# Centroids turned raw and scaled in place, first loads on two queues, and a new order of the early work

## The chip, the cores and the metric

The kernel runs on one core of a Trainium2 chip. The metric is the device time of one execution in microseconds (us). Three runs of the kernel before gave 226.42, 226.63 and 226.57 us, median 226.57 us. One more execution was profiled; it took 227.3 us, of which the profile's span covers 225.3 us.

## The reference

Tokens attend only to tokens of the same cluster; the cluster is the nearest of 16 centroids of the head by cosine. Its output goes through a feed-forward layer (softmax-linear activation, normalisation, output product).

```python
c_n = centroids / (np.linalg.norm(centroids, axis=-1, keepdims=True) + 1e-06)
q_assign = np.argmax(np.einsum('bhsd,hcd->bhsc', q_n, c_n), axis=-1)
k_assign = np.argmax(np.einsum('bhsd,hcd->bhsc', k_n, c_n), axis=-1)
mask = q_assign[:, :, :, None] == k_assign[:, :, None, :]
scores = np.where(mask, scale * np.matmul(q, k.transpose(0, 1, 3, 2)), -1000000000.0)
attn = softmax(scores)
x = (attn @ v), heads side by side          # 3072 tokens x 512
h = x @ w_in                                # 512 x 1024
solu = h * softmax(h)
out = (layernorm(solu) * g_ln) @ w_out      # 1024 x 512
```

Batch 4, 8 heads, 768 tokens, head size 64, all in float32.

## The kernel before

The work goes by head pairs: 4 batches of 4 pairs, named `b.p`. For each pair the kernel loads q and k rows (`raw`), turns them so that the 64 head components lie on partitions (`xt`), multiplies them with the normalised centroids (`csc`, the "cluster product"), turns that back (`cst`), takes the maximum per token (`mx`), makes a one-hot row (`oh`), turns it again (`oht`) and copies it into 16 partitions below the cast q and k in `qk`. With these rows under them the score product `sps` gives masked scores in one pass. ACT takes the exponential (`e`), PE multiplies with v (`ops`), DVE divides by the sum (`x`), and the feed-forward layer follows for 128 tokens at a time (`hreg`, `u`, `yps`).

Nothing is scheduled by the compiler. Every step has a short name and stands in a table (`ORDER`), one list per engine, written out by hand; a second table (`AWAY`) says which steps run on an engine other than their usual one. Each engine issues its list strictly in that order, and semaphores make a step wait for its inputs. The names that matter here:

- `cn`: the norms of the 128 centroid rows, and before the change the scaled rows `c_n` (L877 to L890). `cp`: PE turns `c_n` into `cps` (L899). `cf`: DVE multiplies that with a 0/1 mask `own` into `c_by_two` (L903), the centroid operand of the first five pairs, which lies in `w_out_c`. `cq`, `cb`: the same again into `c_bd` (L910), for the later pairs.
- `tp`: three transposes of q or k on PE into one of three banks of `hreg` (L402); `xa`: the copy of such a bank to `xt` (L409), by DVE or ACT. A fourth `tp` must wait until the `xa` of the first has emptied its bank.
- `ca`: the casts into `qk` (L454 to L458). `cl`: the cluster product (L471). `tb`, `mx`, `oh`, `ot`: its way back (L485, L498, L504, L520). `pl`: the copy of the one-hot rows into `qk` (L532).
- Pair 0.0 is done in halves: the first head's tokens run through `tp`, `cl` to `pl` alone, so that its scores can begin before the second head is ready. The halves are called 0 and 1 below.
- `S`, `E`, `V`, `N`: one bank of scores (two matmuls, L637), its exponential (L643), one value product (six matmuls, L660), one division (L685). Scores have three PSUM banks, so the fourth S waits for the first E.
- `wm` and `fl`: matmuls on zeros whose result is not used (`idle_p`, L854). They stand where PE would wait otherwise.
- `gt` (L594): a small transpose that stands after the 14th S; here it is a milestone, since all that follows it stands in the same order in both kernels.

Of the kernel before, what the change touches and what calls it, by code (L numbers as in the profile page):

```python
# [22 lines left out]
class Weave:  # L23
# [6 lines left out]
        ld4 lv si ld6 lv ld lg lv ld2 lo2 lv lo ld2 lo ld6 li4 tx ld lv ld6 lv tx lv tu ld5 lv ld tx  # L30
        ld tu ld tu ld8 ou ld tu ou ld4 lv ld7 lv ld tu ld4 ou tx ld tu ld4 ou tx ld5 ou ld tu ld2
        lv ld tu ld tx ld4 ou ld3 ou pl ld5 tu lv ld4 lv tu ou tu ld3 lv ou tx ld lv tu ld2 pl ou tx
        ld2 ou pl tu ou lv tx tu pl ou tu2 tx2 tu ou tx2 tu ou tu ou tx tu ou tu ou tu ou6
    """
    ORDER["POOL"] = """
        zo po =ca0.0.0.1.0 ca =pl0.0.0.1.1 pl cv =ca0.1.0.1 =ca0.1.0.0 =pl0.0.1.0.0 pl z
        =pl0.0.1.0.1 ca pl ca =cv0.1.1 =ca0.2.1.1 pl =ca0.2.0.1 pl2 ca2 =ca0.3.1.1 cv =pl0.2.0.0
        =ca0.3.1.0 cv pl =ca0.3.0.1 z pl =cv0.3.1 =ca1.0.0.0 cv =ca1.0.1.0 pl =z4 gs z ca =pl1.0.1.1
        sg ca =pl1.0.0.1 pl2 wi4 =ca1.1.1.0 =cv1.0.1 =ca1.1.0.1 cv =ca1.1.1.1 =at1 =ca1.2.0.1 at ca
        al =pl1.1.1.1 cv =pl1.1.0.0 pl bl pl ca z =ca1.2.1.1 al at ca cv =pl1.2.1.1 =pl1.2.0.0 al  # L40
        =pl1.2.0.1 pl =ca2.0.1.0 bl cv =ca1.3.0.1 at =cv1.3.1 =ca1.3.1.0 ca al =pl1.3.1.1 =pl1.3.0.0
        pl cv bl pl =cv2.1.0 ca =pl2.0.0.0 pl =at5 pl2 at al =ca2.0.1.1 =ca2.1.0.0 =pl2.1.0.1
        =ca2.1.1.1 ca cv al =ca2.3.0.0 bl cv =pl2.1.1.1 =ca2.2.0.1 =ca2.1.1.0 =pl2.1.0.0 =ca2.2.0.0
        pl bl =ca2.3.1.1 at2 al =ca2.2.1.0 cv ca cv pl =ca2.3.1.0 pl at pl =pl2.3.1.1 =pl2.3.1.0 ca
        pl at pl al =ca3.0.0.0 ca =ca3.0.1.0 bl ca =cv2.3.1 al =ca3.1.1.1 cv =pl3.0.0.0 =pl3.0.1.1
        pl bl =ca3.2.0.1 al ca =cv3.0.1 cv pl at2 ca al =pl3.1.1.1 =ca3.3.0.0 =ca3.2.0.0 =cv3.1.1
# [5 lines left out]
        wm fl2 tp fl2 tp fl8 cp tp fl7 cl tp fl11 cl fl16 tp S tp S cq S2 tp S tp2 S V S tp V S tp  # L52
# [33 lines left out]
    """  # L86
    AWAY = {}
    AWAY.update(dict.fromkeys("""
        ca0.0.0.0.0 ca0.0.0.1.1 ca1.3.1.1 sc23.0 tu22.1 tu23.1 xa0.0.1.0 xa0.2.1.0 xa0.2.1.1
        xa0.3.0.0  # L90
    """.split(), "ACT"))
    AWAY.update(dict.fromkeys("""
# [1203 lines left out]
```

## Time and profile before

| what | value |
|---|---|
| median of three runs | 226.57 us |
| profiled execution, whole | 227.3 us |
| its span | 225.3 us |
| PE busy | 219.2 us (97%) |
| DVE busy | 200.3 us (89%) |
| ACT busy | 191.3 us (85%) |
| POOL busy | 127.7 us (57%) |
| first score matmul starts | 10.82 us |
| first exponential starts | 11.25 us |

The share of busy time is counted for each engine by itself. PE means matmuls, PEld the loading of their weights, DVE the vector engine, ACT the scalar engine, POOL the GpSimd engine, SP the engine that issues most DMAs; a name with q (SPq, ACTq) is the time that an engine spends on issuing a DMA. The chain of waits is followed back from the last instruction, and shows at each moment what the end was waiting for. In the timeline the columns are start, duration, engine, line, operation, what it writes and reads, and in brackets how long the engine had been idle and who released it. A matmul's duration in the timeline includes its pipeline, so neighbours overlap; the chain of waits shows only the part that moves the end.

### The profile page before, as it was taken

To read this page: it belongs to the slowest core of one execution; us is meant where nothing else is said; L and a number is where in the kernel's file an instruction comes from. 1 tells how busy PE (TensorE), PEld (TensorE's weight loads), DVE (VectorE), ACT (ScalarE), POOL (GpSimd) and SP (SyncE) were. 2 spreads that over 40 slices of the span, in tenths; PEclk is the share of its full clock that TensorE was granted. 3 is DMA by queue.
4 is the path that set the end of the run, shared out by engine and by line. 5 is a ranking of instruction groups with operands and counts; after the bars stand their busy time and mean duration, and the time that the engine had idled before them with its cause. 6 is when DMAs were issued, how large, how long until landed. Compare 5 with 4: busy or idle time off the path is not lost.

```text
span 225.3 us, 6745 instructions
## 1 busy us (share of the span) xinstructions
PE 219.2 (97%) x2501; PEld 146.8 (65%) x2501; DVE 200.3 (89%) x359; ACT 191.3 (85%) x366; POOL 127.7 (57%) x246
## 2 busy tenths in 40 slices
PE   8999999999999999999999999999999999999993
PEld 8877864666666767666566656676666677665452
DVE  2799997899999999999999899898998996879982
ACT  3399988999979999998989979899989899964353
POOL 3379985942385597289995670957965102122341
PEclk9999999999999999999999999999999999999999
DMA  5999994289999999799997998789771724659522
GB/s 182 366 370 354 196 243 191 47 163 220 187 179 153 213 179 169 148 161 175 184 219 155 147 215 149 180 170 162 175 166 58 93 28 116 90 155 177 166 83 103
DMA packets 117327, 38.80 MB, mean 172 GB/s; under 512 B 105640, under 2 KB 112816, under 8 KB 117296
## 3 DMA queue, kind: packets, MB, share of 16 engines
q1 hardware_dynamic: 117008, 38.06, 79.0%
q8 instruction: 19, 0.31, 0.6%
q10 hardware_dynamic: 288, 0.33, 0.4%
q14 instruction: 12, 0.10, 0.2%
HBM read 23.11 MB, written 6.29 MB: 130 GB/s over the span
## 4 chain that ended last, share of the span: by engine, by line
PE 80%; DVE 10%; ACT 2%; POOL 2%; issue 2%; DMA 1%; SPq 1%; DVEq 0%; ACTq 0%; POOLq 0%
PE sps L637 23%; PE hreg L746 16%; PE yps L810 16%; PE ops L660 12%; PE hreg L402 3%; PE csc L476 3%; PE idle_p L854 3%; DVE xt L427 2%; ACT e L643 2%; PE csc L471 1%; DMA raw<-in_q_dram 1%; DVE nmax L752 1%; DVE y L827 1%; DVE oh L510 1%; PE hreg L609 1%
## 5 line engine op out<-in xcount | busy, mean ns | idle before, releaser
L643 ACT ACTIVATE e<-sps 128x512 bf16<-128x512 f32 x288 | 150.6, 610 | 10.5 <-PE sps L637 8.6
L637 PE MATMUL sps<-qk 80*128 80x256 bf16 (+3 forms) x648 | 98.9, 260 | 0.3
L637 PEld LDWEIGHTS <-qk 80*128 80x128 bf16 (+1 forms) x648 | 52.1, 97 | 32.0 <-issue 8.6
L660 PEld LDWEIGHTS <-e 128*128 128x128 bf16 x1152 | 52.5, 97 | 16.0 <-issue 4.0
L660 PE MATMUL ops<-v,e 128*128 128x65 bf16 x1152 | 58.7, 193 | 0.5 <-DVE x L685 0.3
L746 PE MATMUL hreg<-w_in_sb,xT 128*128 128x512 bf16 x192 | 54.4, 379 | 0.0
L810 PE MATMUL yps<-w_out_c,uT 128*128 128x512 bf16 x184 | 49.9, 379 | 0.3 <-DVE y L827 0.3
L765 DVE TENSOR_TENSOR u<-e_sb,hreg 128x1024 bf16<-128x1024 bf16 (+1 forms) x25 | 29.1, 1166 | 5.0 <-ACT e_sb L758 4.9
L758 ACT ACTIVATE e_sb<-hreg,nmax 128x1024 bf16<-128x1024 f32 x24 | 26.8, 1118 | 6.7 <-DVE nmax L752 6.5
L776 DVE BATCH_NORM_STATS2 bs<-u 128x6 f32<-128x512 bf16 x48 | 31.6, 676 | 0.3
L550 POOL COPY qk<-oht 32x384 f32<-32x384 f32 x40 | 20.6, 515 | 18.8 <-DVE oht L523 14.9
L752 DVE TENSOR_REDUCE nmax<-hreg 128x1 f32<-128x1024 f32 x24 | 28.9, 1203 | 1.3 <-PE hreg L746 1.1
L456 POOL CAST qk<-xt 64x768 bf16<-64x768 f32 (+1 forms) x31 | 25.5, 823 | 6.9 <-DVE xt L409 3.0
L458 POOL TENSOR_SCALAR qk<-xt 64x768 bf16<-64x768 f32 (+1 forms) x28 | 23.4, 836 | 4.0 <-PE yps L810 2.3
L810 PEld LDWEIGHTS <-uT 128*128 128x128 bf16 x200 | 17.8, 97 | 11.5 <-ACT uT L742 0.8
L746 PEld LDWEIGHTS <-xT 128*128 128x128 bf16 x192 | 16.5, 97 | 8.1 <-issue 0.6
L792 POOL TENSOR_SCALAR esq<-es,mv 128x1 f32<-128x1 f32 x24 | 8.1, 339 | 22.6 <-DVE mv L780 22.0
L427 DVE STREAM_TRANSPOSE xt<-raw 128x768 f32<-128x768 f32 x22 | 20.9, 959 | 0.0
L685 DVE TENSOR_TENSOR x<-ops,den 128x256 bf16<-128x256 f32 (+1 forms) x39 | 18.9, 486 | 1.3
L786 POOL TENSOR_SCALAR es<-esum 128x1 f32<-128x1 f32 x24 | 5.6, 239 | 23.3 <-ACT e_sb L758 14.9
L568 POOL CAST v<-vf 128x384 bf16<-128x384 f32 x27 | 14.3, 532 | 7.7 <-DMA vf<-in_v_dram 4.7
L795 POOL TENSOR_TENSOR alpha<-esq,halves 128x1 f32<-128x1 f32 x24 | 13.4, 560 | 2.0
(82 smaller groups left out, 186.6 us busy)
## 6 DMA issues: line engine op xcount, KB each, us to landing
vf<-in_v_dram SPq DMA_DIRECT2D x16, 384.0 KB, 4.4
out_dram<-y SPq DMA_DIRECT2D x23, 256.0 KB, 2.8
raw<-in_q_dram SPq DMA_DIRECT2D x44, 96.0 KB, 3.2
raw<-in_k_dram SPq DMA_DIRECT2D x44, 96.0 KB, 3.4
w_g<-in_moe_w_out_dram SPq DMA_DIRECT2D x4, 512.0 KB, 8.0
w_st<-in_moe_w_in_dram SPq DMA_DIRECT2D x4, 512.0 KB, 6.9
raw<-in_q_dram SPq DMA_DIRECT2D x4, 384.0 KB, 7.2
raw<-in_k_dram SPq DMA_DIRECT2D x4, 384.0 KB, 7.8
```

The source lines that it names most:

```text
L427: nc.vector.transpose(xt[:], raws[b, p, i][:].rearrange("p j c -> p (j c)"))
L456: VEC[e].tensor_copy(dst, src)
L458: VEC[e].tensor_scalar(dst, src, scalar1=inv_C, scalar2=1.0, op0=Alu.mult, op1=Alu.mult)
L637: nc.tensor.matmul(sps_[n, k][:, c0:c0 + w], side(b, h // 2, 1, h % 2, keys)[r], side(b, h // 2, 0, h % 2, slice(s0 * P, s0 * P + w))[r])
L643: nc.scalar.activation(es[n, k][:, :w], sps_[n, k][:, :w], Act.Exp, scale=exp_scale, bias=-exp_scale)
L660: nc.tensor.matmul(opss[g][:, s, :VW], es[n, k][:, c0:c0 + P], v1[slot(b, h // 2)][:, h % 2, kt, :VW], start=(kt == 0), stop=(kt == n_t - 1))
L746: uses(nc.tensor.matmul(hreg[:, at(f, f2)[1], :], xTs[f][:, dc, :], w_in_sb[:, dc, f2 * FF2:(f2 + 1) * FF2], start=(dc == 0), stop=(dc == ...
L752: uses(nc.vector.tensor_reduce(ff[f, "nmax"][:], pair_of(f), axis=AXY, op=Alu.max, negate=True), *both(f))
L758: uses(nc.scalar.activation(ff[f, "e"][:], pair_of(f), Act.Exp, bias=ff[f, "nmax"][:], accum_out=ff[f, "esum"][:]), *both(f))
L765: uses(nc.vector.tensor_tensor(ff[f, "u"][:, at_], ff[f, "e"][:, at_], pair_of(f)[:, at_], op=Alu.mult), *banks)
L776: nc.vector.bn_stats(ff[f, "bs"][:, f2, :], ff[f, "u"][:, f2, :])
L810: ins = nc.tensor.matmul(dst, ff[f, "uT"][:, at(f, f2)[0] * (n_fc // 2) + c, :], w_out_c[:, fc, cols], start=(fc == chunks[0]), stop=(fc = ...
```

## The change

The centroids are no longer scaled before they are turned. Their 128 raw rows are loaded twice, side by side, one copy by SP's queue and one by ACT's. PE turns them as soon as they are there; ACT copies the result to SBUF (`ct`, tile `c_t`). The norms run beside that. PE then multiplies a 128x128 broadcast of the inverse norms with the identity, which spreads them along the free axis on all partitions (`ci`). DVE multiplies both into the blocks of `c_by_two` and `c_bd` that are not zero; POOL has zeroed the whole tiles before. The blocks of heads 0 and 1 come first (`cg`), those of heads 2 to 7 (`cf`) and `c_bd` (`cb`) later. One small DVE step of the norm now does not depend on the one in front of it. The scaled rows `c_n`, the mask `own`, the second transpose `cq` are gone. Core of the diff:

```diff
-    nc.sync.dma_start(out=c_all[:], in_=centroids.rearrange("h c d -> (h c) d"))
+    for x, e in enumerate((nc.sync, nc.scalar)):
+        e.dma_start(out=c_two[:, x, :], in_=centroids.rearrange("h c d -> (h c) d"))
     for hh in range(2):
         for i in range(2):
-            load_head(0, 0, i, hh, nc.sync if i or hh else nc.scalar)
+            load_head(0, 0, i, hh, nc.sync if i else nc.scalar)
...
+    nc.gpsimd.memset(c_by_two, 0.0)
+    nc.gpsimd.memset(c_bd[:], 0.0)
...
-    nc.vector.scalar_tensor_tensor(out=c_r0[:], in0=c_r0[:], scalar=c_nsq[:], in1=c_s0[:],
+    nc.vector.tensor_scalar(c_s1[:], c_s0[:], scalar1=2e-6, scalar2=None, op0=Alu.add)
+    nc.vector.scalar_tensor_tensor(out=c_norm[:], in0=c_r0[:], scalar=c_nsq[:], in1=c_s1[:],
                                    op0=Alu.mult, op1=Alu.add)
-    nc.vector.tensor_scalar(c_norm[:], c_r0[:], scalar1=0.5, scalar2=1e-6,
-                            op0=Alu.mult, op1=Alu.add)
     nc.vector.reciprocal(c_inv[:], c_norm[:])
-    nc.vector.tensor_scalar(c_n[:], c_all[:].unsqueeze(1).to_broadcast([P, 2, D]),
-                            scalar1=c_inv[:], scalar2=None, op0=Alu.mult)
-    add("wm", "PE", 3.55, -1000, lambda e: [idle(P) for _ in range(26)])
+    add("wm", "PE", 3.55, -1000, lambda e: [idle(P) for _ in range(18)])
...
+    def spread_inverse():
+        nc.tensor.matmul(cs["t"][:, 1, :], c_inv[:].to_broadcast([P, P]), ident_f[:])
+
+    def keep_blocks(dst, lo, hi, step):
+        for x in range(2):
+            r = slice(x * D, (x + 1) * D)
+            src = [y.rearrange("p (h c) -> p h c", c=NC_) for y in (c_t[r], cs["t"][r, 1, :])]
+            hs = slice(lo + (x if step == 2 else 0), hi, step)
+            nc.vector.tensor_tensor(dst[r, :, x * NC_:(x + 1) * NC_], src[0][:, hs], src[1][:, hs],
+                                    op=Alu.mult)
+
+    add("cp", "PE", 0.42, 0, lambda e: turn_centroids(), [])
+    add("ct", "ACT", 0.3, -600, lambda e: nc.scalar.copy(c_t[:], cs["t"][:, 0, :]), ["cp", "wa"])
+    add("ci", "PE", 0.42, 0, lambda e: spread_inverse(), ["cn", "cp"])
+    add("cg", "DVE", 0.25, -500, lambda e: keep_blocks(c_by_two[:, 0:2], 0, 2, 1), ["ci", "ct"])
+    add("cf", "DVE", 0.3, -490, lambda e: keep_blocks(c_by_two[:, 2:H], 2, H, 1), ["ci", "ct"])
+    add("cb", "DVE", 0.3, -480, lambda e: keep_blocks(c_bd[:], 0, H, 2), ["ci", "ct"])
```

The turned centroids and the spread norms share the PSUM tile of the value products (`ops`), so the first V now waits for `cf` and `cb`. A `pl` of half 0 and one `xa` of half 1 go to ACT; the one-hot step takes its engine from the table, and still runs on DVE everywhere. The tables move the early work, up to `gt`; behind it all lists are as before. The start of PE's list before and after:

```diff
-        wm fl2 tp fl2 tp fl8 cp tp fl7 cl tp fl11 cl fl16 tp S tp S cq S2 tp S tp2 S V S tp V S tp
-        cl V S tp2 S V S2 V tp S V S gt tp S2 cl S2 V2 S V S tp S V S V S tp S V S cl S2 V S V3 S2
+        wm fl2 cp fl6 tp2 ci tp fl2 cl tp fl8 cl fl10 S2 tp2 S2 tp4 S3 tp cl tp S2 V tp S V3 S2 V tp
+        S V S gt tp S2 cl S2 V2 S V S tp S V S V S tp S V S cl S2 V S V3 S2 tp2 S V S V2 S tp S V S2
```

First place, ACT's list from its start. Before it issues one load, and copies three of the four `hreg` banks of pair 0.0:

```order
L384 DMA raw<-in_q_dram 128x384
L860 ACT_TABLE_LOAD
L860 ACTIVATE warm<-halves 128x1
L409 COPY xt<-hreg 128x384 x3
L454 ACTIVATE qk_99<-xt 64x3x128 x2
L643 ACTIVATE e<-sps 128x512 x6
L454 ACTIVATE qk_99<-xt 64x3x128 x2
L643 ACTIVATE e<-sps 128x512
L409 COPY xt<-hreg 128x384
```

After the change:

```order
L842 DMA c_two<-in_centroids_dram 128x64
L382 DMA raw<-in_q_dram 128x384 x2
L861 ACT_TABLE_LOAD
L861 ACTIVATE warm<-halves 128x1
L916 COPY c_t<-cps 128x128
L407 COPY xt<-hreg 128x384 x2
L452 ACTIVATE qk_99<-xt 64x3x128
L407 COPY xt<-hreg 128x384 x2
L452 ACTIVATE qk_99<-xt 64x3x128
L536 COPY qk_99<-oht 16x2x3x64
L452 ACTIVATE qk_99<-xt 64x3x128
L643 ACTIVATE e<-sps 128x512 x4
```

ACT now issues three loads ahead of its table load, copies all four banks of pair 0.0 and the turned centroids, and takes one `pl` (L536) from POOL.

Second place, DVE's list from the `pl` of half 0 to the copies of pair 0.1. Before:

```order
L532 COPY qk_99<-oht 16x2x3x32 x2
L485 STREAM_TRANSPOSE cst<-csc 128x192
L409 COPY xt<-hreg 128x384
L498 TENSOR_REDUCE mx<-cst 128x12
L409 COPY xt<-hreg 128x384
L910 TENSOR_TENSOR c_bd<-cps,own 128x128
L568 CAST v_0_105<-vf 128x6x64
L504 TENSOR_TENSOR w_out_c<-cst,mx 128x6x2x16
L409 COPY xt<-hreg 128x384
L520 STREAM_TRANSPOSE oht<-w_out_c 128x384
L409 COPY xt<-hreg 128x384 x3
```

After the change:

```order
L536 COPY qk_99<-oht 16x2x3x32 x2
L483 STREAM_TRANSPOSE cst<-csc 128x192
L911 TENSOR_TENSOR w_out_c<-c_t,cps 64x6x16 x2
L911 TENSOR_TENSOR c_bd<-c_t,cps 64x4x16 x2
L496 TENSOR_REDUCE mx<-cst 128x12
L407 COPY xt<-hreg 128x384 x4
L502 TENSOR_TENSOR w_out_c<-cst,mx 128x6x2x16
L568 CAST v_0_105<-vf 128x6x64
L518 STREAM_TRANSPOSE oht<-w_out_c 128x384
L407 COPY xt<-hreg 128x384 x2
```

Six copies stand there in both. Four small block products (L911) take the place of one product (L910), and four copies now stand in a row ahead of the one-hot step of half 1.

Third place, PE's list from its first scores. Before:

```order
L402 MATMUL hreg<-ident_f,raw 128x128 x3
L637 LDWEIGHTS qk_99
L637 MATMUL sps<-qk_99 128x256
L637 LDWEIGHTS qk_99
L637 MATMUL sps<-qk_99 128x256
L402 MATMUL hreg<-ident_f,raw 128x128 x3
L637 LDWEIGHTS qk_99
L637 MATMUL sps<-qk_99 128x256
L637 LDWEIGHTS qk_99
L637 MATMUL sps<-qk_99 128x256
L899 MATMUL cps<-ident_f,c_n 128x128
```

After the change, from the third score bank on (two banks and two `tp` stand ahead):

```order
L637 LDWEIGHTS qk_99
L637 MATMUL sps<-qk_99 128x256
L637 LDWEIGHTS qk_99
L637 MATMUL sps<-qk_99 128x256
L637 LDWEIGHTS qk_99
L637 MATMUL sps<-qk_99 128x256
L637 LDWEIGHTS qk_99
L637 MATMUL sps<-qk_99 128x256
L400 MATMUL hreg<-ident_f,raw 128x128 x12
```

The scores now go in twos and threes, and four `tp` (12 transposes) stand in one row, which is more than the three banks hold.

More of the change, by code (lines that the diff above doesn't have):

```diff
@@ L38 @@
[L38 to L43, printed above, removed]
@@ L1037 @@
                 e = ("DVE", "POOL")[j % 2] if half else "POOL" if apart(b, p) else "SP"
-                costs = ({"DVE": 0.3, "POOL": 0.41} if half else
+                costs = ({"DVE": 0.3, "POOL": 0.41, "ACT": 0.46} if half else
                          {"POOL": 0.76, "DVE": 0.46} if apart(b, p) else
@@ L1226 @@
             add(f"ou{f}", "SP", 0.54, s + 8, (lambda e, f=f: f_out(f)), [f"sc{f}"], move=0.8)
-    for name, eng, busy in (("cn", "DVE", 4.66), ("wa", "ACT", 4.3), ("po", "POOL", 3.7),
+    for name, eng, busy in (("cn", "DVE", 4.66), ("po", "POOL", 3.7),
                             ("si", "SP", 3.95)):
```

159 lines of the change are left out of this document (76 added, 83 removed).

## The prediction

> **What bounds the kernel now.** First the page, for the share of each engine:
>
> ```profile
> span 225.3 us, 6745 instructions
> PE 219.2 (97%) x2501; PEld 146.8 (65%) x2501; DVE 200.3 (89%) x359; ACT 191.3 (85%) x366; POOL 127.7 (57%) x246
> ```
>
> PE is nearly full, but part of its early work is filler, so the share alone says nothing of the start. There the chain of waits is read (start, length, what):
>
> ```profile
> 0.97 3.17 PE idle_p L854 x28
> ...
> 4.14 0.64 PE hreg L402 x3
> ...
> 4.99 0.64 PE hreg L402 x3
> 5.63 0.85 PE idle_p L854 x8
> 6.49 0.21 PE cps L899
> 6.70 0.41 PE hreg L402 x3
> ...
> 7.50 0.46 PE csc L471 x8
> ...
> 8.44 0.61 PE idle_p L854 x11
> 9.05 0.47 PE csc L471 x8
> ...
> 10.53 0.33 PE hreg L402 x3
> 10.86 0.35 PE sps L637 x2
> ...
> 11.54 0.22 PE sps L637 x2
> ...
> 19.50 0.15 PE gps L594
> 19.65 0.48 PE hreg L402 x3
> ```
>
> The chain stays on PE, but up to 10.53 us it is mostly fillers: PE waits there for data, in disguise. What follows stands in a fixed order; a lead won before 10.5 us reaches the end if every engine that is full in between can take it. The windows tell who is full (us from:to, length, then busy time of PE, PEld, DVE, ACT, POOL):
>
> ```profile
> 10.50:19.40 8.90, 8.90 (x104) 6.96 (x102) 8.70 (x18) 8.03 (x17) 6.91 (x13) 1.00 1.08 361
> 19.40:26.10 6.70, 6.70 (x87) 4.72 (x87) 6.09 (x14) 6.65 (x14) 6.18 (x10) 1.00 1.04 302
> 26.10:34.70 8.60, 8.22 (x125) 6.24 (x124) 8.28 (x19) 7.78 (x16) 7.61 (x16) 1.00 0.90 227
> ```
>
> PE is busy all the time to 26.1 us, and DVE for 8.70 of 8.90 us in the first of these: two engines carry the early stage together. DVE's timeline gives the rest:
>
> ```profile
> 4.70 0.16 DVE L889 RECIPROCAL c_inv<-c_norm 128x1 f32<-128x1 f32 x1
> ...
> 6.74 0.42 DVE L903 TENSOR_TENSOR w_out_c<-cps,own 128x256 f32<-128x256 f32 x1
> ...
> 8.03 0.38 DVE L485 STREAM_TRANSPOSE cst<-csc 128x192 f32<-128x192 f32 x1 [0.33 <-PE csc L471]
> ...
> 9.92 0.58 DVE L532 COPY qk<-oht 16x192 f32<-16x192 f32 x2
> 10.53 0.38 DVE L485 STREAM_TRANSPOSE cst<-csc 128x192 f32<-128x192 f32 x1
> 10.90 0.56 DVE L409 COPY xt<-hreg 128x384 f32<-128x384 f32 x1
> 11.37 0.34 DVE L498 TENSOR_REDUCE mx<-cst 128x12 f32<-128x192 f32 x1
> ...
> 12.10 0.28 DVE L910 TENSOR_TENSOR c_bd<-cps,own 128x128 f32<-128x128 f32 x1
> 12.29 0.35 DVE L568 CAST v<-vf 128x384 bf16<-128x384 f32 x1
> ...
> 26.13 0.58 DVE L485 STREAM_TRANSPOSE cst<-csc 128x384 f32<-128x384 f32 x1 [0.29 <-PE csc L471]
> ```
>
> From 8.03 us, where it waits 0.33 us for the first cluster product, DVE's next wait for PE comes at 26.13 us, and is 0.29 us.
>
> **Step 1: the first cluster product, 1.08 us earlier.** PE's new list up to it, by the rows above: 20 fillers instead of 28 at 3.17/28 = 0.113 us end at 0.97 + 2.26 = 3.23; cp 0.21 gives 3.44; six fillers at 0.85/8 = 0.106 give 4.08; two tp (0.64 each) 5.36; ci, of cp's shape and so 0.21, 5.57; the third tp 6.21; two fillers 6.42. Cluster product at 6.42 instead of 7.50. What it also needs is ready: c_inv ends at 4.86 (4.70 + 0.16), ahead of ci at 5.36; the two products of cg start 0.04 after ci (cf started at 6.74, 0.04 after cps), and by the rows of L903 and L910 (256 elements 0.42, 128 elements 0.28, so 1.1 ns an element and 0.14) cost 0.17 each for 32 elements: done at 5.96. ACT's copy of the second tp takes 0.48 and is done at 5.9:
>
> ```profile
> 4.82 0.48 ACT L409 COPY xt<-hreg 128x384 f32<-128x384 f32 x1 [2.15 <-PE hreg L402]
> 10.03 0.73 POOL L532 COPY qk<-oht 16x192 f32<-16x192 f32 x2 [1.76 <-DVE oht L520]
> 11.25 3.12 ACT L643 ACTIVATE e<-sps 128x512 bf16<-128x512 f32 x6 [1.33 <-PE sps L637]
> ```
>
> The ct copy (a third of that copy) runs at 3.5 to 3.9 in ACT's idle time: the bracket of the first row shows 2.15 us of it.
>
> The loads must be there. Landing times, one row each from the issue:
>
> ```profile
> c_all<-in_centroids_dram SPq DMA_DIRECT2D x1, 32.0 KB, 2.4
> raw<-in_q_dram ACTq DMA_DIRECT2D x1, 192.0 KB, 2.7
> raw<-in_k_dram SPq DMA_DIRECT2D x1, 192.0 KB, 2.7
> raw<-in_q_dram SPq DMA_DIRECT2D x1, 192.0 KB, 3.4
> ```
>
> ```profile
> 0.72 0.41 ACTq L384 DMA_DIRECT2D raw<-in_q_dram  x1
> 1.17 1.28 ACT L860 ACT_TABLE_LOAD   x1 [1.17 <-PEq L1280]
> ```
>
> On ACT's queue the first q load is now second, issued about 1.15 instead of 0.72: it lands near 1.15 + 2.7 = 3.9, used at 4.08. The centroids land at 0.72 + 2.4 = 3.1, used at 3.23. The second q load, issued at about 1.6 as before, lands at 5.0, used at 5.57. Two more issues at 0.41 push ACT's table load to 2.0, its end to 3.3, still ahead of ct. SP loses one early issue, so all its later loads move up by some 0.45, and the 4 KB of g slips in between: nothing there. The tightest margin is 0.2 us.
>
> **Step 2: the first scores, 1.3 us earlier.** From the cluster product to DVE's last pl the order on DVE is the same (8.03 to 10.50), so that ends at 10.50 - 1.08 = 9.42. Before, S waited for POOL's second pl (10.03 + 0.73 = 10.76). That one now runs on ACT, POOL's one ends at 9.3, and ACT's, at the 0.3 to 0.5 us of its other copies, at 9.1 to 9.4. S starts at about 9.5 instead of 10.86. The second cluster product, 1.0 us ahead of its reader before (9.05 + 0.47 against 10.53), loses none of that room.
>
> **Step 3: DVE takes some of it back.** After half 0's pl, DVE does the same work as before (six xa, one ca, cv, the chain of half 1 and of pair 0.1), except that the four block products cf and cb replace one product. That one held DVE for 12.29 - 12.10 = 0.19. By the line above, two of 96 elements and two of 64 take 0.25 and 0.21; less the 0.09 by which the next one overlapped there, 0.55 for all four, without that 0.91. The extra is 0.36 to 0.72; I take 0.52, near the middle, since one row alone shows such an overlap. DVE's lead is 1.08 - 0.52 = **0.55 us** at the end of pair 0.1's chain, and could be 0.29 more at 26.13.
>
> **Step 4: PE.** Up to gt both kernels have the same 14 S, one cl and six V. Before, PE went from S at 10.86 to gt at 19.50 in 8.64; to that come 0.33 for the tp that stood ahead of S, and off go 0.11 to 0.2 for cq. From 9.5 that gives gt at about 18.3. New waits come on top: the four tp in a row need banks that DVE empties at 0.47 apiece (11.37 - 10.90) while a tp takes 0.33, which is 0.14 twice; the tp behind the cluster product of 0.1 needs a copy that DVE now does after half 1's chain, about 0.5. So gt comes at 18.4 to 19.2, 0.3 to 1.1 ahead. Just behind it a tp took 0.48 instead of 0.33 (19.65): PE already waited for DVE there, so it cannot keep more than DVE's lead. ACT's first exponential moves from 11.25 to 10.0, and the six there took 0.52 apiece, so ACT is no tighter than it was.
>
> **Sum.** At 26.1 us both engines lead by 0.55, and from there the order is the old one, the waits are between the engines, and the loads stand far enough ahead. Removed fillers count for nothing by themselves: they covered waiting. The profiled execution took 227.3, 2.0 beyond its span, and would take 226.75; it was 0.73 above the median of the runs shown, so I subtract from the median: 226.57 - 0.55 = **226.0 us**. What a measurement of this kernel can tell from no change is about 0.2%, 0.45 us, so the forecast is barely on the faster side.
>
> **Rivals.**
> *More arrives.* If the block products pitch at 0.55 in all (extra 0.36) and DVE also uses up the 0.29 us wait at 26.13, the lead is 1.08 - 0.36 + 0.29 = 1.0: 225.55 us. For it speaks that PE alone would be up to 1.1 ahead at gt; against it the 0.48 row.
> *It is given back.* Block products at 0.28 each, the whole L910 row, cost 4 x 0.28 - 0.19 = 0.93, and DVE leads by 0.15: 226.4 us, no change. For it: DVE is 98% busy in that window and nothing big was taken off it.
> *The clock comes late: slower.* A filler took 0.106 us in the row at 5.63 and 0.61/11 = 0.055 at 8.44, a tp 0.64 and then 0.41 to 0.33: PE ran at half pace until about 6.5 us, and 72 fillers kept it busy, of which 46 are left. At half pace the cluster product takes 0.92, so from 6.42 the list runs 0.92 + 0.64 (tp) + 0.85 (eight fillers) + 0.92 (second product) to 9.75 and, with ten fillers at 0.106, to 10.8. DVE's chain starts 0.46 later and is 0.62 - 0.52 = 0.1 ahead: the gain is gone and no more. It decides from about 10.8 us on: every us of half pace in the scores then costs 0.5 us, and one lasting to 13.2 costs 1.2, less 0.1 of lead: 227.7 us. Against it: by the list PE has no gap over 0.1 us before 6.4.
> [...]
>
> **How the numbers follow.** Forecast (lead 0.35 to 0.75) 0.45; more arrives 0.18; given back 0.27; late clock 0.10. The forecast's part below 0.45 of lead and most of given back are "same". So faster 0.50, same 0.38, slower 0.12. The range takes in 1.15 of lead (PE's bound at gt) and a late clock that costs a little: 225.4 to 226.9.
>
> **What would show it.** Cluster product near 6.4, first S near 9.5, first E near 10.0: step 1 and 2. Block products between DVE's second L483 and its reduce taking 0.55 to 0.9: step 3. gt at 18.4 to 19.2; the L469 product that releases DVE's transpose at 26.13 before, now about 25.6: step 4. The forecast is wrong if a tp waits for its load, if fillers still take 0.1 us after 7 us, or if PE is idle long in the row of 12 transposes.

## The result, and the profile after

The changed kernel took 228.16 us (median of 20 runs, 226.87 to 230.97), the kernel before on the same chip 226.33 us (20 runs, 225.41 to 228.00): a ratio of 1.0094, 95% interval 1.0069 to 1.0119 (formed from the executions, so not the quotient of the medians). It is slower, and its spread is as much part of the result as its median. On another chip the unaltered changed kernel gave 227.40 against 226.50 us, 1.0033 (1.0011 to 1.0055): slower again, by less. The ratios leave out executions more than 1.5% above the fastest of their kernel, the one of 230.97 here and one of 230.19 there; without them the medians are 228.12 and 227.21 us, and these are used below.

The profiled execution of the changed kernel took 227.04 us, near the lower end of its range, and that of before, 227.3 us, lies near the upper end of its own. Their spans are therefore a poor comparison; a milestone behind the early work, the first maximum of the feed-forward layer on DVE, is a better one.

The page, span and shares:

```profile
span 225.0 us, 6672 instructions
PE 215.5 (96%) x2445; PEld 144.7 (64%) x2476; DVE 200.5 (89%) x361; ACT 192.2 (85%) x369; POOL 127.4 (57%) x243
```

PE is 3.7 us less busy, with 26 fillers fewer among the rest; DVE is as busy as before. The chain of waits of the changed kernel (start, length, what):

```profile
1.16 3.73 DMA raw<-in_q_dram
...
4.94 0.88 PE hreg L400 x6
...
6.61 0.56 PE csc L469 x8
...
10.11 0.25 DVE w_out_c L911
10.36 0.01 issue
10.37 0.26 DVE w_out_c L911
10.64 0.21 DVE c_bd L911
10.87 0.24 DVE c_bd L911
...
18.02 1.10 DVE qk L456
```

Before, this chain ran over PE's fillers. Now it begins with the first q load, which lands at 4.90 us, and from the cluster product to about 20 us it runs mostly over DVE, with the four block products and one cast (`ca`) among its pieces. The first two windows behind the first score matmul (from:to, length, then busy PE, PEld, DVE, ACT, POOL):

```profile
9.74:19.40 9.66, 9.03 (x102) 7.12 (x102) 9.46 (x20) 8.15 (x17) 6.27 (x11) 1.00 1.08 344
19.40:26.10 6.70, 6.51 (x86) 4.60 (x84) 6.52 (x14) 6.30 (x14) 6.17 (x11) 1.00 1.12 299
```

PE, which had no idle time there before, now waits 0.63 us in the first and 0.19 us in the second; DVE stays at 98% in the first and goes from 91% to 97% in the second. The milestone, DVE's timeline of before and then of the changed kernel:

```profile
50.26 1.23 DVE L752 TENSOR_REDUCE nmax<-hreg 128x1 f32<-128x1024 f32 x1
```

```profile
51.11 1.22 DVE L752 TENSOR_REDUCE nmax<-hreg 128x1 f32<-128x1024 f32 x1
```

The first scores began 1.08 us earlier than before (9.74 against 10.82), and 41 us later the changed kernel is 0.85 us behind. The lag stays at 0.84 to 0.85 up to 113 us. (The profiled execution of before then loses 1.07 us against it between 113 and 153 us, where no other profile loses more than 0.6; that is why the spans say otherwise.)

Where DVE lost it, its timeline in the changed kernel:

```profile
9.69 0.38 DVE L483 STREAM_TRANSPOSE cst<-csc 128x192 f32<-128x192 f32 x1
...
11.12 0.35 DVE L496 TENSOR_REDUCE mx<-cst 128x12 f32<-128x192 f32 x1
...
14.00 0.66 DVE L568 CAST v<-vf 128x384 bf16<-128x384 f32 x1
...
17.94 1.18 DVE L456 TENSOR_SCALAR qk<-xt 64x768 bf16<-64x768 f32 x1
...
21.23 0.87 DVE L538 COPY qk<-w_out_c 16x384 f32<-16x384 f32 x1
...
26.43 0.58 DVE L483 STREAM_TRANSPOSE cst<-csc 128x384 f32<-128x384 f32 x1
...
29.25 1.03 DVE L538 COPY qk<-w_out_c 16x384 f32<-16x384 f32 x1
```

and the same cast and copies before:

```profile
15.80 0.53 DVE L458 TENSOR_SCALAR qk<-xt 64x768 bf16<-64x768 f32 x1
...
20.84 0.52 DVE L538 COPY qk<-w_out_c 16x384 f32<-16x384 f32 x1
...
28.95 0.48 DVE L538 COPY qk<-w_out_c 16x384 f32<-16x384 f32 x1
```

The transpose at 9.69 was 0.84 ahead of before (10.53), the reduce behind it at 11.12 only 0.25 (11.37). By its reduce the kernel before had also done one copy of a bank (0.47) and still had its block product (0.19) to do, so on equal work the lead was gone by there. Then four casts and copies that before took 0.35 (at 12.29), 0.53, 0.52 and 0.48 take 0.66, 1.18, 0.87 and 1.03: together 1.86 us more. Block products (1.01 from 10.11 to 11.12, against 0.19 for the one product before, so 0.82 more) and these four make 2.68; the shift from 0.84 ahead to 0.85 behind is 1.69. Of the difference, 0.29 is the wait at 26.13 before, which is gone, and 0.28 a one-hot step (L502, formerly L504) that took 0.98 and now 0.70; 0.42 is not itemised. Part of that is that durations in this timeline overlap: counted from each start to the next one's, the four make 1.73 and not 1.86.

### The profile page after: what moved, and what is told of

It is laid out like the page before. It is cut to its first block, busy times and chain, and to the rows that moved or that the text cites. A ratio compares the mean times of both kernels' runs of the same rounds, so it can differ in the third digit from the quotient of the medians.

```text
span 225.0 us, 6672 instructions
## 1 busy us (share of the span) xinstructions
PE 215.5 (96%) x2445; PEld 144.7 (64%) x2476; DVE 200.5 (89%) x361; ACT 192.2 (85%) x369; POOL 127.4 (57%) x243
## 4 chain that ended last, share of the span: by engine, by line
PE 65%; DVE 15%; DMA 5%; POOL 5%; issue 4%; ACT 3%; SPq 2%; ACTq 0%; DVEq 0%; POOLq 0%
PE sps L637 19%; PE yps L810 14%; PE hreg L746 14%; PE ops L660 11%; DMA raw<-in_k_dram 4%; PE csc L474 2%; ACT e L643 2%; SPq L419 2%; DVE xt L407 2%; POOL qk L454 2%; DMA raw<-in_q_dram 2%; DVE w_out_c L502 1%; DVE u L765 1%; DVE x L685 1%; PE csc L469 1%
## 5 line engine op out<-in xcount | busy, mean ns | idle before, releaser
L643 ACT ACTIVATE e<-sps 128x512 bf16<-128x512 f32 x288 | 150.1, 608 | 10.4 <-PE sps L637 9.2
L746 PE MATMUL hreg<-w_in_sb,xT 128*128 128x512 bf16 x175 | 50.7, 378 | 1.0 <-issue 0.2
L810 PE MATMUL yps<-w_out_c,uT 128*128 128x512 bf16 x170 | 47.1, 379 | 0.5
L568 POOL CAST v<-vf 128x384 bf16<-128x384 f32 x27 | 14.8, 551 | 14.5 <-DMA vf<-in_v_dram 13.6
```

What stands on the lines that cost most here:

```text
L643: nc.scalar.activation(es[n, k][:, :w], sps_[n, k][:, :w], Act.Exp, scale=exp_scale, bias=-exp_scale)
L746: uses(nc.tensor.matmul(hreg[:, at(f, f2)[1], :], xTs[f][:, dc, :], w_in_sb[:, dc, f2 * FF2:(f2 + 1) * FF2], start=(dc == 0), stop=(dc == ...
L810: ins = nc.tensor.matmul(dst, ff[f, "uT"][:, at(f, f2)[0] * (n_fc // 2) + c, :], w_out_c[:, fc, cols], start=(fc == chunks[0]), stop=(fc = ...
```

## The experiments

Fourteen kernels were run, one of them the changed kernel unaltered, each timed beside the kernel before on the same chip (226.50, 226.41, 226.21 and 225.96 us in the four sittings). Differences in us below are between such medians; by the intervals each is good to 0.3 to 0.7 us either way. A profile shows one execution of a kernel, which can lie anywhere in its spread.

### Does a lag at the first scores reach the end?

b_delay, the kernel before with 15 more fillers ahead of its first scores:

```diff
-        wm fl2 tp fl2 tp fl8 cp tp fl7 cl tp fl11 cl fl16 tp S tp S cq S2 tp S tp2 S V S tp V S tp
+        wm fl2 tp fl2 tp fl8 cp tp fl7 cl tp fl11 cl fl31 tp S tp S cq S2 tp S tp2 S V S tp V S tp
```

> The kernel before with 15 more fillers on PE ahead of its first score, 15 x 0.055 = 0.83 us; nothing else is changed. If a lag at the first score reaches the end one to one, the time rises by 0.6 to 0.9 us and L752 stands at 51.0 to 51.1 us. If slack takes it up, it rises by less than 0.3 us. If a lag of this size is amplified later (the loads from 115 to 145 us meeting other transfers), it rises by 1.3 us or more.

227.19 against 226.50 us, ratio 1.0039 (1.0020 to 1.0058). PE's and DVE's timelines:

```profile
11.32 0.38 PE L637 MATMUL sps<-qk 80*128 80x256 bf16 x2
```

```profile
26.75 0.58 DVE L485 STREAM_TRANSPOSE cst<-csc 128x384 f32<-128x384 f32 x1 [0.29 <-PE csc L471]
...
29.23 1.03 DVE L538 COPY qk<-w_out_c 16x384 f32<-16x384 f32 x1
...
51.11 1.23 DVE L752 TENSOR_REDUCE nmax<-hreg 128x1 f32<-128x1024 f32 x1
```

The 15 fillers took 0.83 us, but PE began their row 0.21 earlier than in the profile of before (9.25 against 9.46). The first scores are 0.50 later (10.82), the transpose at 26.75 is 0.62 later (26.13), the first maximum 0.85. So the lag is not taken up on the way. It grows, for a reason of its own: the copy at 29.23 took 1.03 instead of 0.48. In the median 0.69 was lost.

### The first loads

a_again is the changed kernel unaltered. a_loads_back puts the first q load at the head of ACT's queue and the others on SP's, with the second centroid copy behind the q load. b_loads_two is the kernel before with the changed kernel's load order and one centroid copy that nothing reads.

```diff
+    nc.scalar.dma_start(out=c_dup[:], in_=centroids.rearrange("h c d -> (h c) d"))
...
-            load_head(0, 0, i, hh, nc.sync if i or hh else nc.scalar)
+            load_head(0, 0, i, hh, nc.sync if i else nc.scalar)
```

> The changed kernel, unaltered, once more. If its loss has a fixed cause in the kernel, it is again 1.3 to 2.2 us above the kernel before, and its first feed-forward maximum (DVE L752, at 50.26 us before and 51.11 after) stands again at 51.0 to 51.3 us. If the loss came from the day or the chip, it is within 0.5 us of the kernel before. Where the profile loses beside the first 35 us is open: I look whether the step from 100 to 150 us, in which the profiled run of the change gained 1.09 us on that of before, comes out the other way.

> The changed kernel with the first loads as before: the first q load leads ACT's queue, the second centroid copy follows it, the other three q and k loads are on SP. Loads theory (four loads in flight on two queues land together, the first q load at 4.90 instead of 3.42): first q load lands at 3.4 to 3.7, PE's first tp starts at 4.0 to 4.2 instead of 4.94, the first score at 8.9 to 9.2 instead of 9.74, and the time is 0.6 to 0.9 us below that of the change. DVE theory (the vector engine is full from 9 to 30 us and four block products and slowed copies set the loss): the first score comes earlier, but L752 stands within 0.3 us of 51.1, and the time falls by less than 0.4 us.

> The kernel before with only the loads of the change: a second copy of the centroids (to a tile nobody reads) and both q loads on ACT's queue. Loads theory: the first q load lands at 4.8 to 5.0, the first score comes 0.5 to 0.9 us later than 10.82, and the time rises by 0.4 to 0.9 us. DVE theory: less than 0.4 us. If the loss of the change in the middle of the run comes from the lanes that one more load shifts, the time rises by over 1 us.

a_again: the 227.40 us given above. a_loads_back: 228.65 us, 1.0094 (1.0069 to 1.0119), a miss: in its profile the second centroid copy landed late in turn, and PE waited 1.00 us for that at 4.29 instead. b_loads_two: 227.05 us, 1.0034 (1.0005 to 1.0063), spread from 225.88 to 228.74. PE's timeline in it (its profiled execution was the slowest of the twelve):

```profile
4.83 0.88 PE L402 MATMUL hreg<-ident_f,raw 128*128 128x128 f32 x3 [0.69 <-DMA raw<-in_q_dram]
...
9.74 0.86 PE L402 MATMUL hreg<-ident_f,raw 128*128 128x128 f32 x3
```

The load order alone makes PE wait 0.69 us, and a tp at 9.74 still takes 0.86 us; at full pace the same row reads 0.49 to 0.55. So in this execution PE worked at half pace to about 10.4 us, against some 6.5 before. Two effects are mixed here, the wait and the late full pace; the next two kernels cover the wait.

### The wait covered with fillers

a_fill is the changed kernel with 8 more fillers behind the centroids' turn; b_loads_two_fill is b_loads_two with 8 more in its first row.

```diff
-        wm fl2 cp fl6 tp2 ci tp fl2 cl tp fl8 cl fl10 S2 tp2 S2 tp4 S3 tp cl tp S2 V tp S V3 S2 V tp
+        wm fl2 cp fl14 tp2 ci tp fl2 cl tp fl8 cl fl10 S2 tp2 S2 tp4 S3 tp cl tp S2 V tp S V3 S2 V tp
```

> The changed kernel with eight more fillers on PE behind the centroid transpose, 8 x 0.106 = 0.85 us, which cover its wait for the first q load (0.80 us in the profile of the change). Nothing else. Clock theory (that wait makes the half-pace stage last longer in many executions: in one profile of the change the fillers still took 0.09 us at 9.1 us): all executions run at full pace from 6 to 7 us on, the slow ones (229 to 231 us) are gone, the spread falls under 2 us, the median stands 0.2 to 0.9 us above the kernel before. Vector-engine theory alone: the fillers change nothing, spread and median stay as in the two groups of the change (0.9 and 1.8 us above).

> The kernel before with the two-queue loads and eight fillers ahead of its first tp, which cover its wait of 0.69 us. Clock theory: without them the executions fell into a group at 225.9 to 226.7 and one at 228.3 to 228.7 us; with them the upper group is gone and the median is within 0.5 us of the kernel before. If the upper group has another cause (lanes, the later loads), it stays.

a_fill: 227.37 us, 1.0043 (1.0025 to 1.0061), none above 228.56 where the changed kernel reached 230.25 on the first chip and 228.67 on the second. b_loads_two_fill: 227.09 us, 1.0040 (1.0017 to 1.0062), no better than without, and its upper times, 227.0 to 228.3, did not go away as the expectation had it. In both profiles full pace came by 5 us, and a_fill's first scores came at 9.37, the earliest so far; still its first maximum is 0.48 after before (50.74) and its median 0.96 above. So covering the gap at PE does not remove the loss. It does not fix the time of full pace either: in the profile of a_fill_pool, below, with the same list of PE, that came only after 6.4 us.

### Loads as before, block products on POOL

a_one_copy takes the loads exactly as before; POOL makes the second centroid copy from the first on the chip, and PE's early fillers are one more (two more ahead of the centroids' turn, one fewer behind it). a_one_copy_pool also moves cf and cb to POOL, which reads a copy of the spread norms made by ACT; the first V then waits for that copy instead of cf and cb. a_fill_pool is a_fill with the same move. a_one_copy_pool_ca also puts the slow cast `ca` back ahead of its pair's transpose.

```diff
+    nc.gpsimd.tensor_copy(c_two[:, 1, :], c_two[:, 0, :])
...
-    add("cf", "DVE", 0.3, -490, lambda e: keep_blocks(c_by_two[:, 2:H], 2, H, 1), ["ci", "ct"])
+    add("cr", "ACT", 0.3, -495, lambda e: nc.scalar.copy(c_r[:], cs["t"][:, 1, :]), ["ci"])
+    add("cf", "POOL", 0.6, -490, lambda e: keep_blocks(c_by_two[:, 2:H], 2, H, 1, e), ["cr", "ct"])
...
-        cn cg ca tb mx oh ot pl2 tb mx xa4 oh cv ot xa2 tb mx oh ca ot N gk =xa0.3.1.0 pl xa
+        cn cg ca tb mx oh ot pl2 tb mx xa4 oh cv ot xa2 ca tb mx oh ot N gk =xa0.3.1.0 pl xa
```

(The first line is a_one_copy's, the next three the POOL move's, the last two a_one_copy_pool_ca's.)

> The changed kernel with the first loads exactly as before; the second centroid copy is made on the chip by POOL from the first (about 0.25 us), and three fillers are added. Loads theory: first q load lands at 3.4 to 3.6, no wait of PE over 0.3 us ahead of 6 us, pace full from about 6.5, first score at 8.8 to 9.2 us, and the maximum of L752 at 50.2 to 50.5 (before 50.26, change 51.11), so the time is within 0.4 us of the kernel before. Vector-engine theory: the first score comes earlier all the same, but L752 stays at 50.8 or later.

> As the last one, and the four later block products (cf, cb; 1.01 us on DVE in the profile of the change, against 0.19 for the product that they replace) go to POOL, which is idle there, from an SBUF copy of the spread norms made by ACT (0.27 us). Vector-engine theory: L752 comes 0.6 to 1.0 us earlier than in the last kernel, and the time falls by as much, to 0.4 to 1.0 us below the kernel before. If PE or the loads set the early stage, under 0.3 us.

> The changed kernel with its two queues of first loads, eight more fillers ahead of the first tp, and the block products cf and cb on POOL instead of DVE (from a copy of the spread norms that ACT makes). With the fillers alone it measured 0.96 us above the kernel before. Vector-engine theory: DVE's 0.97 us of block products is what the changed kernel lost, so this is 0.8 to 1.2 us below that: 226.2 to 226.6 us, a ratio of 0.999 to 1.001 to the kernel before, and DVE's reduce of half 1 starts within 0.3 us of its transpose's end instead of 1.0. Rival (the late q load and the clock alone cost the time): the products' place is of no account and it stays at 227.2 to 227.5 us.

> The kernel with the first loads as before, the second centroid copy made on the chip and the block products on POOL (226.29 us, level with the kernel before), and one cast of pair 0.1 (ca, 1.18 us on DVE at 17.4) put back ahead of that pair's transpose tb, as its place was before the change. Collision theory: it took 1.18 instead of 0.53 us because POOL runs its own ca at the same time; in its old place it takes 0.5 to 0.6 us and the kernel is 0.3 to 0.6 us below that one: 225.7 to 226.0 us. Rival (PE or ACT takes up what DVE gains, or the cast is slow there too): 226.2 to 226.4 us, no change.

a_one_copy: 227.72 us, 1.0063 (1.0039 to 1.0086). PE's and DVE's timelines of its profiled execution (226.82 us):

```profile
9.19 0.60 PE L637 MATMUL sps<-qk 80*128 80x256 bf16 x4 [0.31 <-DVE qk L536]
```

```profile
50.59 1.23 DVE L752 TENSOR_REDUCE nmax<-hreg 128x1 f32<-128x1024 f32 x1
```

Its first scores are 1.63 us ahead of before, more than the 1.3 of the prediction, and the first maximum is 0.33 behind: the lead was lost between, where DVE has the same block products and slow casts as the changed kernel. This execution is one of three near 226.7; the other seven took 227.6 to 228.3, so the median holds something that this profile does not show.

a_one_copy_pool, on the same chip: 226.29 us, 1.0006 (0.9984 to 1.0028), level with before and not below it as expected. Taking the block products off DVE was worth 1.43 us there, clear of noise (1.0063 against 1.0006). a_fill_pool: 226.68 against 226.21 us, 1.0023 (1.0005 to 1.0042). It is 0.47 above before, where a_fill, on another chip, was 0.96 above, so the same move was worth about 0.5 there, half of what was expected; as the two intervals overlap, this second difference alone is not shown.

a_one_copy_pool_ca: 226.68 against 226.21 us, 1.0024 (1.0000 to 1.0048), not better than without, against the collision theory's 0.3 to 0.6. DVE's timelines say why, first that of a_one_copy_pool, then this one's:

```profile
17.68 1.18 DVE L456 TENSOR_SCALAR qk<-xt 64x768 bf16<-64x768 f32 x1
...
29.00 1.04 DVE L538 COPY qk<-w_out_c 16x384 f32<-16x384 f32 x1
```

```profile
15.05 0.53 DVE L456 TENSOR_SCALAR qk<-xt 64x768 bf16<-64x768 f32 x1
...
20.11 0.35 DVE L538 COPY qk<-w_out_c 16x384 f32<-16x384 f32 x1
...
24.32 0.20 DVE L672 RECIPROCAL den<-ops 128x6 f32<-128x6 f32 x1 [0.24 <-PE ops L660]
...
25.40 0.58 DVE L483 STREAM_TRANSPOSE cst<-csc 128x384 f32<-128x384 f32 x1 [0.29 <-PE csc L469]
...
26.49 0.88 DVE L568 CAST v<-vf 128x384 bf16<-128x384 f32 x1
...
28.40 1.03 DVE L538 COPY qk<-w_out_c 16x384 f32<-16x384 f32 x1
```

The cast takes 0.53 again, as the theory had it, and the copy at 20.11 takes 0.35 where it took 0.88. But what DVE gains there PE takes up, as the rival had it: DVE now waits for PE by 0.24 us at 24.32 and by 0.29 at 25.40, and had no such wait in a_one_copy_pool. From the first scores (9.62) to the transpose at 25.40 this kernel takes 15.78 us, a_one_copy_pool 15.89 (10.27 to 26.16). Behind it the cast at 26.49 takes 0.88 instead of 0.71, the copy at 28.40 is as slow as it was, and the first maximum comes at 50.27, 0.01 behind before.

### One cause at a time, in the kernel before

b_dve adds three block products of the changed kernel's shapes to DVE, with results that nothing reads. b_gap and b_cold take fillers out of PE's first row (18 and 1 are left of 26). b_gap_more is b_gap with fewer fillers about the centroids' turn and DVE's centroid product moved ahead of a cast.

```diff
+        for k in (6, 6, 4):
+            nc.vector.tensor_tensor(c_x[0:D, 0:k], ident_f[0:D, 0:k * NC_].rearrange("p (k c) -> p k c", c=NC_),
+                                    s[:, 0:k], op=Alu.mult)
...
-    add("wm", "PE", 3.55, -1000, lambda e: [idle(P) for _ in range(26)])
+    add("wm", "PE", 3.55, -1000, lambda e: [idle(P) for _ in range(18)])
...
-        wm fl2 tp fl2 tp fl8 cp tp fl7 cl tp fl11 cl fl16 tp S tp S cq S2 tp S tp2 S V S tp V S tp
+        wm fl2 tp fl2 tp fl3 cp tp fl3 cl tp fl11 cl fl16 tp S tp S cq S2 tp S tp2 S V S tp V S tp
...
-        cn ca cf xa tb mx oh ot =pl0.0.0.0.1 pl tb xa mx xa cb cv oh xa ot xa =xa0.2.0.1 xa ca tb mx
+        cn cf ca xa tb mx oh ot =pl0.0.0.0.1 pl tb xa mx xa cb cv oh xa ot xa =xa0.2.0.1 xa ca tb mx
```

(The first three lines are b_dve's, the next two b_gap's and b_gap_more's, with `range(1)` in b_cold; the rest is b_gap_more's.)

> The kernel before with three more small products behind the c_bd product on DVE (64x96 twice, 64x64 once, results not used), 0.7 to 0.8 us by the changed kernel's rows for this shape. Vector-engine theory: DVE is the bound there, so the first feed-forward maximum comes 0.4 to 0.8 us later and the median is 0.4 to 0.8 us above the kernel before, ratio 1.002 to 1.0035. Rival (waits for PE and ACT behind it take the work up): within 0.2 us of the kernel before.

> The kernel before with 1 instead of 26 fillers in its first row: PE has three small matmuls by 1.3 us and is then idle until its first load lands at about 3.5 us. Clock theory (full pace needs a stretch of unbroken work before it): half pace lasts beyond the 5.9 to 6.5 us of the kernel before in most executions, to 8 us or later; fillers then take 0.1 us in the rows of 11 and 16, the first score matmul comes at 10.5 to 12 instead of 10.2, and the median is 0.3 to 1.5 us above the kernel before, with a spread of more than 2 us. Rival (the pace changes at a fixed time, whatever PE did): as with 18 fillers, 0.2 to 0.5 us below the kernel before, spread about 1.2 us.

> The kernel before with 18 instead of 26 fillers in its first row: PE is idle about 0.9 us ahead of its first tp at 4.1 us, and nothing else changes. Clock theory: the gap puts off the release of PE's full pace in part of the executions, by 1 to 4 us; fillers after 7 us then still take 0.1 us, the first score matmul comes 0 to 1.0 us later, and the median is 0.2 to 1.0 us above the kernel before with a wider spread. Rival (a gap in the fillers is harmless, the lost time is all DVE's): the median stays within 0.2 us of the kernel before and the spread is the same.

> The kernel before with 18 instead of 26 fillers in its first row (0.37 us below the kernel before by itself), 3 instead of 8 fillers ahead of the centroids' turn, 3 instead of 7 behind it, and DVE's centroid product ahead of its first cast. The first cluster product moves from 6.8 to 6.0 to 6.3 us and the first score matmul from 10.2 to 9.5 to 9.8, with the vector engine's work unchanged. If a lead at the start arrives where DVE gets no more work: 0.6 to 0.9 us below the kernel before, 225.3 to 225.7 us on a chip where that takes 226.2 to 226.5. Rival (PE is limited by something else by 26 us, or the fewer fillers put off the full pace): no better than 0.4 us below it, or a second group of times 1 us higher.

b_dve: 226.57 against 225.96 us, 1.0017 (1.0002 to 1.0032). DVE's timeline:

```profile
12.15 0.76 DVE L915 TENSOR_TENSOR c_x<-ident_f,cps 64x96 f32<-64x96 f32 x3
...
51.03 1.23 DVE L752 TENSOR_REDUCE nmax<-hreg 128x1 f32<-128x1024 f32 x1
```

0.76 us of work on DVE, and the first maximum 0.77 later than before. The agreement is partly chance: DVE's half 1 began 0.15 earlier here (10.38 against 10.53), the transpose at 26.13 before came 0.55 later (26.68), so up to there 0.70 of the 0.76 arrived, and the copy at 29.17 again took 1.03 instead of 0.48. Waits behind it take up next to nothing.

b_cold: 227.20 against 225.96 us, 1.0050 (1.0027 to 1.0073), spread from 225.59 to 228.53. PE's timeline (profiled execution 227.59 us):

```profile
0.97 0.50 PE L854 MATMUL idle_p<-w_out_c 128*128 128x128 bf16 x3 [0.97 <-DVE halves L858]
3.52 0.87 PE L402 MATMUL hreg<-ident_f,raw 128*128 128x128 f32 x3 [2.04 <-DVE c_nsq L877]
...
7.62 0.87 PE L471 MATMUL csc<-xt,w_out_c 128*32 128x192 f32 x8
...
9.12 1.00 PE L854 MATMUL idle_p<-w_out_c 128*128 128x128 bf16 x11
10.05 0.53 PE L471 MATMUL csc<-xt,w_out_c 128*32 128x192 f32 x8
...
11.75 0.38 PE L637 MATMUL sps<-qk 80*128 80x256 bf16 x2
```

The first product of eight takes 0.87 us at 7.62, the second 0.53 at 10.05: full pace came at about 9.5 us (of the 11 fillers at 9.12, at 0.106 or 0.055 each, about four were slow), 3 us later than before, with the same loads and the same work behind the fillers. First scores 0.93 later, median 1.24 higher. The rival, a pace that changes at a fixed time, does not fit this profile, nor the loss in the median.

b_gap: 225.84 against 226.21 us, 0.9981 (0.9966 to 0.9996). A loss of 0.2 to 1.0 us was expected, on a wrong premise: that PE would be idle to 4.1 us. PE's timeline:

```profile
3.52 0.88 PE L402 MATMUL hreg<-ident_f,raw 128*128 128x128 f32 x3 [0.23 <-DVE c_nsq L877]
...
10.20 0.39 PE L637 MATMUL sps<-qk 80*128 80x256 bf16 x2
```

The first tp started at 3.52, 0.41 earlier than before (3.93 in the same view), behind a gap of only 0.23: the q load had been there since about 3.4, and what held the tp before was the fillers themselves. Full pace came at about 5.8, no later than before.

b_gap_more: 225.46 against 225.96 us, 0.9972 (0.9957 to 0.9987). PE's and DVE's timelines:

```profile
6.63 0.57 PE L471 MATMUL csc<-xt,w_out_c 128*32 128x192 f32 x8
...
10.07 0.39 PE L637 MATMUL sps<-qk 80*128 80x256 bf16 x2
```

```profile
49.50 1.23 DVE L752 TENSOR_REDUCE nmax<-hreg 128x1 f32<-128x1024 f32 x1
```

The cluster product and the first scores came 0.3 later than hoped, the gain is 0.50 instead of 0.6 to 0.9, and yet the first scores 0.75 earlier (10.07 against 10.82) arrive as 0.76 at the first maximum. In b_gap 0.62 (10.20) arrived as 0.41 (49.85), with the copy at 27.99 taking 1.03. b_gap_more is faster than both kernels. It has the norms, the operands and DVE's work of the kernel before.

### One stretch in all profiles

The profiles of both kinds of kernel can be laid side by side in one stretch, from the first scores on PE to the first maximum on DVE (us, from their timelines):

| kernel | first scores | first maximum | between |
|---|---|---|---|
| before | 10.82 | 50.26 | 39.44 |
| b_gap_more | 10.07 | 49.50 | 39.43 |
| b_gap | 10.20 | 49.85 | 39.65 |
| b_delay | 11.32 | 51.11 | 39.79 |
| b_loads_two | 12.86 | 52.65 | 39.79 |
| b_loads_two_fill | 10.78 | 50.44 | 39.66 |
| b_cold | 11.75 | 51.30 | 39.55 |
| b_dve | 10.68 | 51.03 | 40.35 |
| changed | 9.74 | 51.11 | 41.37 |
| a_again | 11.12 | 52.52 | 41.40 |
| a_loads_back | 11.07 | 52.48 | 41.41 |
| a_fill | 9.37 | 50.74 | 41.37 |
| a_one_copy | 9.19 | 50.59 | 41.40 |
| a_fill_pool | 10.69 | 51.26 | 40.57 |
| a_one_copy_pool | 10.27 | 50.87 | 40.60 |
| a_one_copy_pool_ca | 9.62 | 50.27 | 40.65 |

With the block products on DVE the stretch takes 41.4 us, whatever the order of the loads, the fillers and the time of full pace. With them on POOL it takes 40.6, so they cost 0.8. What is left above the old order's 39.4 to 39.8, another 0.8 to 1.2, comes with the rest of the new order.

## Why the prediction was wrong

It said 226.0 us (225.4 to 226.9) and faster, and gave slower a chance of 0.12; 228.16 was measured. Step by step:

- **Step 1, first cluster product at 6.42.** The profiled execution came near it (6.61), by luck. The first q load, put at 3.9 with a margin of 0.2, landed at 4.90, and PE had a gap of 0.80. But full pace came at once behind the gap, so the six transposes of two tp took 0.88 and not the 1.28 of the sum, and the rest up to the product 0.79 and not 1.06. Where full pace came later, as in a_loads_back, the cluster product came at 7.86. The time of 2.7 for a load was read where the four first loads were issued one after the other, from 0.72 to 2.10. Now all four are issued between 1.16 and 1.65, and they take 3.5 to 4.3 (medians below). b_loads_two shows that the new order of loads does this by itself (the first q load took 3.5 there); whether the queue, the place in it or the short time between the issues does it is not shown.

```profile
raw<-in_q_dram ACTq DMA_DIRECT2D x2, 192.0 KB, 4.0
raw<-in_k_dram SPq DMA_DIRECT2D x2, 192.0 KB, 3.8
```

- **Step 2, first S at about 9.5.** 9.74 in that execution, and 9.37 with the wait covered. Right where full pace comes early: one list of PE with one order of loads gave 9.19 in a_one_copy's profile and 10.27 in a_one_copy_pool's, where it came at about 7.2 us.
- **Step 3, DVE gives back 0.52 and leads by 0.55.** This is the step that failed. The extra of the block products is 0.82, above the whole range of 0.36 to 0.72: they do not overlap at all (0.25, 0.26, 0.21 and 0.24 in the chain). And "the same work as before" was true of the list, not of its durations: four casts and copies took 1.86 us more, as they began beside POOL's (rows in the last section). Three of them belong to the new order: they read 0.66, 1.18 and 0.87 or 0.88 in all seven profiles that keep their places, and 0.35 to 0.37, 0.53 and 0.52 or 0.53 in all eight of the old order. The last, 1.03 instead of 0.48, took 1.03 in five of these eight as well, among them b_gap and b_dve, so it goes by the phase between DVE and POOL: there it began 0.06 us after a POOL cast, in before and b_gap_more, where it took 0.48 and 0.47, 0.62 after it. Together the lead forecast at 0.55 became a lag of 0.85: some 0.24 was missing at half 1's transpose already (0.84 instead of 1.08), and 1.17 went in this step. That the step fails by itself is seen in the last table: the loss between first scores and first maximum is the same with the loads of before (a_one_copy) and with the wait covered (a_fill). In the median a_one_copy is 1.31 above before, and with the block products off DVE it is level (226.29 against 226.41).
- **Step 4, gt at 18.4 to 19.2.** 19.47, level with before, since it could keep no more than DVE's lead, as that step itself said. The transpose forecast for 25.6 came at 26.43. PE was idle for 0.36 us in the row of 12 transposes and for 0.27 behind it, both times for DVE.
- **The rival "it is given back"**, with a chance of 0.27, had the price of the block products nearly right (an extra of 0.93, measured 0.82), but not the longer casts, and so ended at no change.
- **The rival of the late clock** probably had too small a chance at 0.10. "By the list PE has no gap over 0.1 us before 6.4" rested on the landing time of step 1, and of the signs of a wrong forecast "a tp waits for its load" came true. The profiled execution of the changed kernel does not show this rival, its full pace was early; that of a_loads_back does, with half pace to about 8 us. b_cold shows a late full pace by itself in the kernel before, 1.24 us in the median, with half pace to about 9.5 us in its profile; the rival had 1.1 for one lasting to 13.2, which no run shows: the longest in a profile was to about 10.4 (b_loads_two). The granted clock in the windows does not show it, it stands at 1.00 there; the durations do (a filler 0.106 us, then 0.055).
- **"Removed fillers count for nothing"** was wrong both ways: 25 fewer cost 1.24 us in b_cold, and 8 fewer gained 0.37 in b_gap, where they had held up a tp whose data lay ready. In the chain of waits of before, "PE waits there for data, in disguise" was thus not so for the last 0.4 us ahead of the first tp.

How the loss divides: in the profiles the stretch between first scores and first maximum is 1.6 to 2.0 us longer than in the old order, and 0.8 of that are the block products on DVE. In the medians they are worth 1.43 by one pair (a_one_copy against a_one_copy_pool) and 0.5, not clear of noise, by the other (a_fill against a_fill_pool). The other 0.8 to 1.2 of the stretch is not divided by a run. One tp more stands behind the first scores now (0.33), and the three casts and copies meet POOL's; but taking the slowest cast out of its collision gained nothing, since PE was next to hold DVE up. The median of the changed kernel (1.79 above before) is worse than its profile (0.85 at the first maximum). The late full pace in other executions (half pace to about 9.5 us in a_again's profile, that of 230.19 us, which the medians leave out) is the likely rest by the author's estimate, and its share stays open between about 0 and 0.8: with the wait covered a_fill is still 0.96 above, and the changed kernel itself was 0.71 above on the other chip.

## What to carry to other kernels

Where one engine is full behind the place that is made earlier, add up what that engine gains or loses in the whole stretch, including casts that a new order brings beside another engine's (here one of 0.53 us became 1.18); the lead at the start says little. Size fillers by when the data landed and not by when the last filler ended: those that run past it hold the work up (the first tp came 0.41 us earlier in b_gap), and a gap ahead of it can put off full pace (from about 6.5 to 9.5 us in b_cold, behind one of 2.04). And read a load's time together with the loads issued beside it: the first q load took 2.7 us in the old order and 3.7 in the new one.

## What the hardware showed that was not expected

**Casts on DVE beside POOL.** POOL's timeline in the changed kernel, at the places of DVE's slow casts and copies:

```profile
17.58 1.13 POOL L456 TENSOR_SCALAR qk<-xt 64x768 bf16<-64x768 f32 x1
...
21.07 0.82 POOL L454 CAST qk<-xt 64x768 bf16<-64x768 f32 x1
...
29.18 0.82 POOL L454 CAST qk<-xt 64x768 bf16<-64x768 f32 x1
```

They end at 18.71, 21.89 and 30.00; DVE's cast and copies, begun meanwhile, end 0.41, 0.21 and 0.28 later (19.12, 22.10, 30.28). In the kernel before the two copies (20.84 and 28.95) also began inside a POOL cast, only later in it, and ended 0.22 and 0.28 after it. The cast at 14.00 in the changed kernel began inside a POOL cast too (13.82 to 14.44) and ended 0.22 after it. So in these six rows the end follows the end of POOL's instruction and not their own start: the copies took 0.87 and 1.03 us where they began 0.16 and 0.07 after POOL's cast, and 0.52 and 0.48 where they began 0.52 and 0.62 after it. Whether DVE stands still meanwhile or runs slower is not shown. DVE's copies out of PSUM (L407) kept their 0.5 us: those at 22.13 and 24.28 in the changed kernel, begun while POOL ran two copies (21.95 to 23.03) and two casts (23.88 to 25.95), took 0.56 and 0.55.

**When full pace comes.** Counted from the start of unbroken work on PE, full pace came about 3.3 us later in the profile of a_fill (0.97 to 4.2), 5.5 in that of before (0.97 to 6.5), 5.6 in that of b_loads_two (4.83 to 10.4), 6.0 in that of b_cold (3.52 to 9.5) and 6.2 in that of a_one_copy_pool (0.97 to 7.2). It is not one length of work: a_fill_pool, with a_fill's list of PE, started it at 0.97 as well, and its fillers and transposes ran at half pace to 6.4. Nor does a gap settle it: in the changed kernel's own profile one of 0.80 us ended at 4.94, and full pace was there at once; in a_again's, the same kernel, one of 0.75 ended at 4.89, and full pace came at about 9.5. What sets the moment is not shown by these runs.
